# A kernel of attention and capacity-limited MoE: a tail of its own for the last batch, and other PSUM banks for the gather

## The chip, the cores and the metric

One NeuronCore of a Trainium2 chip runs the whole program; the other cores are not used. The metric is the device time of one execution in microseconds (us). Engines are TensorE (PE; its weight loads are shown as PEld), VectorE (DVE), ScalarE (ACT), GpSimd (POOL) and SyncE (SP). Each runs its own queue in order, and semaphores tie them together.

## The reference

For each of 8 batches and 12 heads, attention with squared relu in place of softmax; the heads side by side are `x`. Then, in each batch, the 128 tokens of 448 that score highest against `w_gate` go through a two-layer FFN, and the result, scaled by the sigmoid of the score, is added to their rows.

```python
# q, k, v: (8, 12, 448, 64)
scores = scale * np.matmul(q, k.transpose(0, 1, 3, 2))
attn = np.maximum(scores, 0.0) ** 2 / S
attn_out = np.matmul(attn, v)
x = np.ascontiguousarray(attn_out.transpose(0, 2, 1, 3)).reshape(B, S, H * D)   # (8, 448, 768)

scores = np.einsum('bsd,d->bs', x, w_gate)
out = x.copy()
for b in range(B):
    top_idx = np.argpartition(-scores[b], capacity)[:capacity]                  # capacity 128
    xe = x[b, top_idx]
    h = np.maximum(xe @ w1, 0.0)                                                # w1: 768 x 1024
    ye = h @ w2                                                                 # w2: 1024 x 768
    g = 1.0 / (1.0 + np.exp(-scores[b, top_idx]))
    out[b, top_idx] = x[b, top_idx] + g[:, None] * ye
```

## The kernel before

A tile `t` is one pair of heads of one batch: 48 tiles, six a batch (`t = 6*b + hp`). Inputs are loaded on the GpSimd queue two batches ahead, cast to bf16 on the way. For each tile TensorE transposes q and k into `t_ps`, VectorE copies them out (`qkt`, L172); TensorE makes four chunks of scores (`s_ps`, L182 and L186), ScalarE takes the relu (`r_sb`, L194), VectorE squares it (`a_sb`, L195); TensorE multiplies by v (`o_ps`, L206), one tile behind the scores, and ScalarE writes the result as one of six slices of `xT_sb` (L212), the batch's x with its features on the partitions.

The MoE of a batch is cut into steps that are placed between the attention work of later batches. Two tables give the places: there are twelve half steps `hs` a batch, two a tile. `RANK` serves batch b-1 while batch b's attention runs, `FFN` serves batch b-2. The schedule is written out by hand: each engine executes its instructions in the order in which the Python code issues them. The rank steps are:

- `gate`: six matmuls with `w_gate` repeated, into `sc_ps`, and ScalarE's copy to `bc` (the scores, in all partitions).
- `columns`: four tiny matmuls into `col_ps`, VectorE's copy `cols`, and four small VectorE operations that split each score into three bf16 pieces (`tok`).
- `x_chunk(c)`: six transposes of x into `x_ps` and VectorE's copy to `x_sb`, four times; after the fourth GpSimd issues the write of the batch's `x_sb` to `out`.
- `rank_chunk(c)`: a VectorE instruction with an accumulator counts how many scores are larger (L266), four times.
- `one_hot`: `hot`, a 0/1 matrix of token against rank (L271).
- `select`: four matmuls into `sel_ps`, then VectorE's `sel`, `idx` (the chosen tokens) and `g` (their scores).
- `gather(half)`: 12 matmuls of `x_sb` with `hot` into `xe_ps`, and ScalarE's cast to `xeT`, twice.

The FFN steps are `hidden(f)`, 8 times six matmuls into `h_ps` with a ScalarE relu to `hT` after every fourth; and `project(half, ...)`, 8 matmuls into `ye_ps` and ScalarE's scaling by `g` into `gye`. After the second half GpSimd issues an indirect DMA that adds `gye` to the chosen rows of `out` (the scatter, L328).

[...] `s_ps` has two tiles of two banks each; `t_ps`, `o_ps`, `ma_ps` and `mb_ps` have one bank each. A bank that is written again must first have been read by whoever used it last. The MoE has `ma` (all rank steps, and the first half of the gather) and `mb` (the second half of the gather, and the whole FFN).

All DMAs of the kernel are issued by GpSimd. Writes to `out` follow one another strictly, each waiting until the one before has landed: x of batch b, scatter of batch b-1, x of batch b+1, and so on; at the end the scatter of batch 6 and that of batch 7 stand one behind the other.

Behind the 48 tiles the last attention is done (`attend(NT - 1, c)`), then `moe(B, hs)` for the twelve half steps, which are the rank steps of batch 7 mixed with the FFN of batch 6 by the same tables, and at last the FFN of batch 7 alone.

Of the kernel before, what the change touches and what calls it, by code (L numbers as in the profile page):

```python
# [8 lines left out]
FP32 = mybir.dt.float32  # L9
BF16 = mybir.dt.bfloat16  # L10
# [10 lines left out]
def kernel(  # L21
# [132 lines left out]
    def transposes(t):  # L154
        b, hp = divmod(t, NHP)
        h0 = 2 * hp
        qs, ks = q_sb[b % NBUF], k_sb[b % NBUF]
        ps = t_ps_pool.tile([128, S + 512], BF16, name="t_ps")
        for c in range(NC):
            for hh in range(2):  # L160
                nc.tensor.matmul(out=ps[64 * hh:64 * hh + 64, c * P:(c + 1) * P],  # L161
                                 lhsT=qs[:, h0 + hh, c, :], rhs=ident[:P, :P],
                                 is_transpose=True, start=(c == 0), stop=False,
                                 skip_group_check=True)
        for c in range(4):
            for hh in range(2):
                nc.tensor.matmul(out=ps[64 * hh:64 * hh + 64, S + c * 128:S + (c + 1) * 128],  # L167
                                 lhsT=ks[:, h0 + hh, c, :], rhs=ident,
                                 is_transpose=True, start=False, stop=(c == 3),
                                 skip_group_check=True)  # L170
        sb = qt_pool.tile([128, S + 512], BF16, name="qkt")
        nc.vector.tensor_copy(out=sb, in_=ps)  # L172
        qkt[t] = sb

    def scores(t, c):
        sb = qkt[t]
        ps = s_ps_pool.tile([128, 2, 512], FP32, name="s_ps")
# [20 lines left out]
    def attend(t, c):  # L198
        b, hp = divmod(t, NHP)
        vs = v_sb[b % NBUF]  # L200
        if c == 0:
            o_ps[t] = o_ps_pool.tile([128, S], FP32, name="o_ps")
# [15 lines left out]
    def moe_rank(b):  # L218
        xTb = xT.pop(b)
# [23 lines left out]
        def columns():  # L243
# [5 lines left out]
            nc.vector.tensor_copy(out=cols, in_=col_ps)  # L249
            nc.vector.tensor_copy(out=tk[:, :, 2], in_=cols)  # L250
# [24 lines left out]
        def select():  # L275
            sel_ps = ma_ps_pool.tile([CAP, 5], FP32, name="sel_ps", tag="m")
# [8 lines left out]
        def gather(half):  # L285
            xe = (ma_ps_pool, mb_ps_pool)[half].tile([128, 3, CAP], FP32, name="xe_ps", tag="m")
# [6 lines left out]

        steps = {
            "gate": gate, "col": columns, "x": x_chunk, "rank": rank_chunk,
# [4 lines left out]
    def moe_ffn(b, idx, g, xeT):  # L300
# [4 lines left out]
        def hidden(f):  # L305
            if f % 4 == 0:
                ps["h"] = mb_ps_pool.tile([128, 4, CAP], FP32, name="h_ps", tag="m")
# [7 lines left out]
        def project(half, f0, f1):  # L315
            cols_d = slice(half * 384, half * 384 + 384)
            if f0 == 0:
                ps["y"] = mb_ps_pool.tile([CAP, 384], FP32, name="ye_ps", tag="m")
                if half == 0:
                    nc.scalar.activation(out=g, in_=g, func=AF.Sigmoid)  # L320
# [3 lines left out]
            if f1 == NF:  # L324
                nc.scalar.activation(out=gye[:, cols_d], in_=ps["y"], func=AF.Copy,  # L325
                                     scale=g[:, 0:1])
                if half == 1:
                    nc.gpsimd.indirect_dma_start(  # L328
                        out=out.rearrange("b s d -> (b s) d"),
                        out_offset=bass.IndirectOffsetOnAxis(ap=idx[:, :1], axis=0),  # L330
                        in_=gye, in_offset=None, element_offset=b * S * HD,
                        compute_op=ALU.add)

        return {"h": hidden, "y": project}


# [4 lines left out]
        1: [("gate", 0, 6)], 2: [("col",)], 3: [("x", 0)], 4: [("x", 1), ("rank", 0)],  # L341
# [25 lines left out]
    with tc.manual_schedule():  # L367
        transposes(0)
        transposes(1)
        for t in range(NT):  # L370
# [17 lines left out]
            moe(b, 2 * hp + 1)  # L388
        for c in (0, 1, 3, 2):
            attend(NT - 1, c)  # L390
        for hs in range(12):
            moe(B, hs)
        ffn_steps[B - 1] = moe_ffn(B - 1, *handed.pop(B - 1))
        for hs in range(12):
            place(FFN, ffn_steps[B - 1], hs)
# [35 lines left out]
```

## Time and profile before

| | us |
|---|---|
| median of 3 runs | 269.62 (269.57 to 269.96) |
| profiled execution | 268.7 |
| its span, first to last instruction | 266.6 |
| TensorE busy | 211.8 (79%) |
| ScalarE busy | 196.1 (74%) |
| VectorE busy | 179.8 (67%) |
| GpSimd busy | 88.2 (33%) |

The profile is of one execution, and its instructions' times are counted from the start of the span. No engine is busy all the time, so the shares of busy time do not name the bound. The views to read are the chain of work that ended last, the list of waits in the steady part, and the engines' instructions in order of time at the places that the change touches: one boundary between batches (203 to 216 us) and the tail (from 233 us). An entry such as `[0.81 <-DVE sel L280]` says that the engine stood idle for 0.81 us just before, and that a VectorE instruction of line 280 ended the wait. A matmul's length includes its pipeline: of a row with many, the length divided by the count is near the time from one to the next.

### The profile page before, as it was taken

Reading aid. Unit: us, or ns where it says so; the run is one execution under the profiler, and the core shown is the slowest. Engines: PE = TensorE matmul, PEld = TensorE weight load, DVE = VectorE, ACT = ScalarE, POOL = GpSimd, SP = SyncE. Lnnn points to the kernel's source line nnn. Section 1 sums busy time; section 2 is a strip of 40 time slices with the busy share of each in tenths; the row PEclk is TensorE's granted clock in tenths of the full one; section 3 lists DMA queues with packets and bytes.
Section 4 is the critical chain, followed back from the end, with each engine's and each line's share of the span. In section 5 each row is a group of like instructions: output and inputs, shape, how many; then the busy total and the mean of one; then the engine's idle time right before and its main releaser. Section 6 shows DMA issues by size and latency. Waiting matters only on the chain.

```text
span 266.6 us, 6187 instructions
## 1 busy us (share of the span) xinstructions
PE 211.8 (79%) x2496; PEld 126.8 (48%) x2496; DVE 179.8 (67%) x426; ACT 196.1 (74%) x306; POOL 88.2 (33%) x128
## 2 busy tenths in 40 slices
PE   1297740797798988899889988998899889888740
PEld 1143310253466545565556555655565556366620
DVE  3067850289958976798679867986798669847100
ACT  1088960288988998899889988998899889952320
POOL 8999500955630003700460046002000200020210
PEclk9999985589999999999999999999999999999995
DMA  3999999999999123994499249924202420242544
GB/s 40 104 153 122 174 208 200 144 194 198 208 292 192 16 102 111 149 193 117 134 161 190 96 136 166 186 93 137 47 2 81 138 52 0 115 114 42 207 59 59
DMA packets 41723, 34.20 MB, mean 128 GB/s; under 512 B 14944, under 2 KB 39008, under 8 KB 40800
## 3 DMA queue, kind: packets, MB, share of 16 engines
q0 software_dynamic: 41696, 33.83, 75.9%
q8 instruction: 19, 0.31, 0.4%
q14 instruction: 8, 0.07, 0.1%
HBM read 39.32 MB, written 14.16 MB: 201 GB/s over the span
## 4 chain that ended last, share of the span: by engine, by line
DVE 33%; PE 25%; ACT 14%; DMA 11%; POOL 8%; issue 5%; POOLq 1%; ACTq 0%
DVE a_sb L195 15%; ACT r_sb L194 12%; DMA k_sb<-in_k_dram 7%; DVE qkt L172 7%; DVE trash L266 5%; PE xe_ps L290 5%; PE h_ps L309 4%; PE s_ps L182 4%; DVE x_sb L261 4%; PE sc_ps L238 4%; PE o_ps L206 3%; DMA out_dram<-gye,idx 2%; DMA q_sb<-in_q_dram 2%; POOL k_sb L90 2%; POOL k_sb L93 2%
## 5 line engine op out<-in xcount | busy, mean ns | idle before, releaser
L194 ACT ACTIVATE r_sb<-s_ps 128x896 bf16<-128x896 f32 x192 | 147.4, 830 | 28.4 <-PE s_ps L186 14.8
L195 DVE TENSOR_TENSOR a_sb<-r_sb 128x896 bf16<-128x896 bf16 x192 | 104.3, 563 | 38.8 <-ACT r_sb L194 38.5
L182 PE MATMUL s_ps<-qkt 64*128 64x448 bf16 x288 | 47.2, 368 | 7.7 <-ACT r_sb L194 7.5
L206 PE MATMUL o_ps<-a_sb,v_sb 128*64 128x448 bf16 x384 | 49.7, 369 | 1.3 <-DVE a_sb L195 0.3
L172 DVE COPY qkt<-t_ps 128x960 bf16<-128x960 bf16 x48 | 31.2, 650 | 20.7 <-PE t_ps L167 20.7
L161 PE MATMUL t_ps<-ident,q_sb 112*64 112x112 bf16 x384 | 19.1, 221 | 19.1 <-DMA q_sb<-in_q_dram 13.6
L206 PEld LDWEIGHTS <-v_sb 128*64 128x64 bf16 x384 | 20.0, 111 | 28.2 <-issue 21.7
L263 POOL DMA_DIRECT2D out_dram<-x_sb x8 | 4.5, 564 | 86.5 <-DVE x_sb L261 84.6
L161 PEld LDWEIGHTS <-q_sb 112*64 112x64 bf16 x384 | 17.0, 115 | 26.1 <-DMA q_sb<-in_q_dram 18.8
L212 ACT ACTIVATE xT_sb<-o_ps 128x448 bf16<-128x448 f32 x48 | 26.8, 559 | 1.4 <-PE o_ps L206 1.4
L328 POOL DMA_INDIRECT out_dram<-gye,idx x8 | 13.2, 1653 | 43.6 <-ACT xeT L292 26.9
L309 PE MATMUL h_ps<-xeT,w_sb 128*128 128x128 bf16 x384 | 26.5, 219 | 1.3 <-ACT hT L313 0.7
L182 PEld LDWEIGHTS <-qkt 64*128 64x128 bf16 x288 | 11.4, 94 | 32.1 <-issue 29.5
L93 POOL DMA_DIRECT2D v_sb<-in_v_dram x22 | 16.8, 766 | 29.4 <-DMA q_sb<-in_q_dram 20.7
L322 PE MATMUL ye_ps<-w_sb,hT 128*128 128x384 bf16 x128 | 23.5, 327 | 2.1 <-ACT gye L325 1.1
L309 PEld LDWEIGHTS <-w_sb 128*128 128x128 bf16 x384 | 22.6, 98 | 5.1 <-issue 3.2
L167 PE MATMUL t_ps<-ident,k_sb 128*64 128x128 bf16 x384 | 21.2, 228 | 2.4 <-DMA k_sb<-in_k_dram 2.4
L90 POOL DMA_DIRECT2D v_sb<-in_v_dram x22 | 18.7, 848 | 11.0 <-DMA w_sb<-in_moe_w_dram 7.3
L266 DVE SCALAR_TENSOR_TENSOR trash<-bc,cols,tie 112x448 bf16<-112x448 f32 x32 | 21.6, 676 | 0.0
L258 PE MATMUL x_ps<-ident,xT_sb 128*112 128x128 bf16 x192 | 16.8, 223 | 5.4 <-DVE cols L249 5.3
L313 ACT ACTIVATE hT<-h_ps 128x512 bf16<-128x512 f32 x16 | 9.6, 597 | 13.4 <-PE h_ps L309 13.4
L93 POOL DMA_DIRECT2D k_sb<-in_k_dram x22 | 19.0, 865 | 0.4 <-issue 0.4
(54 smaller groups left out, 214.3 us busy)
## 6 DMA issues: line engine op xcount, KB each, us to landing
out_dram<-x_sb POOLq DMA_DIRECT2D x8, 1344.0 KB, 5.2
q_sb<-in_q_dram POOLq DMA_DIRECT2D x6, 672.0 KB, 10.3
w_sb<-in_moe_w_dram POOLq DMA_DIRECT2D x2, 1536.0 KB, 14.8
k_sb<-in_k_dram POOLq DMA_DIRECT2D x12, 192.0 KB, 10.4
v_sb<-in_v_dram POOLq DMA_DIRECT2D x12, 192.0 KB, 7.8
k_sb<-in_k_dram POOLq DMA_DIRECT2D x12, 144.0 KB, 10.3
v_sb<-in_v_dram POOLq DMA_DIRECT2D x12, 144.0 KB, 10.4
q_sb<-in_q_dram POOLq DMA_DIRECT2D x2, 224.0 KB, 4.2
```

Of the source, the lines that this page charges most:

```text
L90: nc.gpsimd.dma_start(out=t[0:64, hs, 0:lo, :], in_=src[b, hs, 0:64 * lo].rearrange("h (p c) d -> p h c d", c=lo))
L93: nc.gpsimd.dma_start(out=t[64:128, hs, 0:hi, :], in_=src[b, hs, 64 * lo:S].rearrange("h (p c) d -> p h c d", c=hi))
L161: nc.tensor.matmul(out=ps[64 * hh:64 * hh + 64, c * P:(c + 1) * P], lhsT=qs[:, h0 + hh, c, :], rhs=ident[:P, :P], is_transpose=True, start ...
L172: nc.vector.tensor_copy(out=sb, in_=ps)
L182: nc.tensor.matmul(out=ps[:, hh, :S], lhsT=sb[rows, S + c * 128:S + (c + 1) * 128], rhs=sb[rows, :S], start=True, stop=True)
L194: nc.scalar.activation(out=r[:, :n], in_=ps[:, :n, :S], func=AF.Relu)
L195: nc.vector.tensor_tensor(out=a[:, :n], in0=r[:, :n], in1=r[:, :n], op=ALU.mult)
L206: nc.tensor.matmul(out=o_ps[t][rows, :], lhsT=vs[:, 2 * hp + hh, c, :], rhs=a[:, hh if c < 3 else 0, :], start=(c == 0), stop=(c == 2), sk ...
L212: nc.scalar.activation(out=xT[b][:, hp, :], in_=o_ps.pop(t), func=AF.Copy, scale=o_scale)
L266: nc.vector.scalar_tensor_tensor(out=trash, in0=bc[:P, :], scalar=cols[:, c:c + 1], in1=tie[:, c, :], op0=ALU.subtract, op1=ALU.is_ge, acc ...
L309: nc.tensor.matmul(out=ps["h"][:, f % 4, :], lhsT=w1_sb[:, m, f * 128:(f + 1) * 128], rhs=xeT[:, m, :], start=(m == 0), stop=(m == NM - 1))
L322: nc.tensor.matmul(out=ps["y"], lhsT=hT[:, f, :], rhs=w2_sb[:, f, cols_d], start=(f == 0), stop=(f == NF - 1))
```

## The change

It has three parts.

1. In every batch, `gather` swaps its banks: the first half goes into `mb`, the second into `ma`. Tags are added so that other tiles can share the pools `t_ps`, `s_ps` and `o_ps`; this alone changes nothing. `columns` is split into `columns` and `pieces`, which the table still places together.
2. The tail is written out by hand. TensorE does five of the six gate matmuls and 20 of the 24 x transposes of batch 7 (`x_begin`, into the two `s_ps` tiles) ahead of the last attention, and the sixth gate matmul, the columns and the last four transposes (`x_end`) behind it. VectorE does the four rank instructions and the one-hot in a row, `pieces` after them. `x_sb` is copied by ScalarE in two large pieces instead of by VectorE in four. Batch 6's FFN follows, its `h` in `mb` and `t`, its `y` in `mb` and `ma`; the gather of batch 7 (`gather_last`, into `o` and `t`, one half cast by each of ScalarE and VectorE) stands between the two `y`, and `select` comes last, into `o`.
3. The FFN of batch 7 (`last`) has its own code: both `h` halves in `s_ps` tiles, the first three feature blocks of four hidden blocks ahead of the other three, the two `y` halves in different banks and interleaved by the halves of `hT`, and the final scaling shared by ScalarE and VectorE.

```diff
@@ moe_rank
-        xTb = xT.pop(b)
+        xTb = xT[b]
...
             nc.vector.tensor_copy(out=cols, in_=col_ps)
+
+        def pieces():
             nc.vector.tensor_copy(out=tk[:, :, 2], in_=cols)
...
-        def select():
-            sel_ps = ma_ps_pool.tile([CAP, 5], FP32, name="sel_ps", tag="m")
+        def select(pool=ma_ps_pool, tag="m"):
+            sel_ps = pool.tile([CAP, 5], FP32, name="sel_ps", tag=tag)
...
         def gather(half):
-            xe = (ma_ps_pool, mb_ps_pool)[half].tile([128, 3, CAP], FP32, name="xe_ps", tag="m")
+            xe = (mb_ps_pool, ma_ps_pool)[half].tile([128, 3, CAP], FP32, name="xe_ps", tag="m")
...
+        def x_begin():
+            for i in range(2):
+                ps["x", i] = s_ps_pool.tile([P, 2, 1024], BF16, name="x_ps2", tag="s")
+                for u in range(2):
+                    for m in range(NM - 1):
+                        x_part(i, u, m)
+
+        def x_part(i, u, m):
+            c = 2 * i + u
+            nc.tensor.matmul(out=ps["x", i][:, u, m * 128:(m + 1) * 128],
+                             lhsT=xTb[:, m, c * P:(c + 1) * P], rhs=ident,
+                             is_transpose=True, start=(m == 0), stop=(m == NM - 1))
+
+        def x_end():
+            for i in range(2):
+                for u in range(2):
+                    x_part(i, u, NM - 1)
+                nc.scalar.copy(out=x_sb[:, 2 * i:2 * i + 2, :], in_=ps["x", i][:, :, :HD])
+            nc.gpsimd.dma_start(out=out[b].rearrange("(p c) d -> p c d", c=NC), in_=x_sb)
+
+        def gather_last():
+            for half, (pool, tag) in enumerate(((o_ps_pool, "o"), (t_ps_pool, "t"))):
+                xe = pool.tile([128, 3, CAP], FP32, name="xe_ps2", tag=tag)
+                for mm in range(3):
+                    m = half * 3 + mm
+                    for c in range(NC):
+                        nc.tensor.matmul(out=xe[:, mm, :], lhsT=x_sb[:, c, m * 128:(m + 1) * 128],
+                                         rhs=hot[:, c, :], start=(c == 0), stop=(c == NC - 1))
+                (nc.scalar.copy if half == 0 else nc.vector.tensor_copy)(
+                    out=xeT[:, half * 3:half * 3 + 3, :], in_=xe)
@@ moe_ffn
+        def last():
+
+            nc.scalar.activation(out=g, in_=g, func=AF.Sigmoid)
+            for half in range(2):
+                h = s_ps_pool.tile([128, 4, CAP], FP32, name="h_ps2", tag="s")
+                for m0 in (0, 3):
+                    for ff in range(4):
+                        f = 4 * half + ff
+                        for m in range(m0, m0 + 3):
+                            nc.tensor.matmul(out=h[:, ff, :],
+                                             lhsT=w1_sb[:, m, f * 128:(f + 1) * 128],
+                                             rhs=xeT[:, m, :], start=(m == 0 and ff == 0),
+                                             stop=(m == NM - 1), skip_group_check=True)
+                f = 4 * half
+                nc.scalar.activation(out=hT[:, f:f + 4, :], in_=h, func=AF.Relu)
+            y = [mb_ps_pool.tile([CAP, 384], FP32, name="y_ps2", tag="m"),
+                 t_ps_pool.tile([CAP, 384], FP32, name="y_ps3", tag="t")]
+            for f0 in (0, 4):
+                for half in range(2):
+                    for f in range(f0, f0 + 4):
+                        nc.tensor.matmul(out=y[half], lhsT=hT[:, f, :],
+                                         rhs=w2_sb[:, f, half * 384:half * 384 + 384],
+                                         start=(f == 0), stop=(f == NF - 1))
+            nc.scalar.activation(out=gye[:, :384], in_=y[0], func=AF.Copy, scale=g[:, 0:1])
+            nc.vector.tensor_scalar(out=gye[:, 384:], in0=y[1], scalar1=g[:, 0:1],
+                                    scalar2=None, op0=ALU.mult)
+            scatter()
@@ behind the 48 tiles
+        last, prev = B - 1, B - 2
+        r, handed[last] = moe_rank(last)
+        f = moe_ffn(prev, *handed.pop(prev))
+        r["gate"](0, NM - 1)
+        r["x_begin"]()
         for c in (0, 1, 3, 2):
             attend(NT - 1, c)
-        for hs in range(12):
-            moe(B, hs)
-        ffn_steps[B - 1] = moe_ffn(B - 1, *handed.pop(B - 1))
-        for hs in range(12):
-            place(FFN, ffn_steps[B - 1], hs)
+        r["gate"](NM - 1, NM)
+        r["col"]()
+        for c in range(NC):
+            r["rank"](c)
+        r["hot"]()
+        r["x_end"]()
+        for i in range(8):
+            f["h"](i, *((mb_ps_pool, "m"), (t_ps_pool, "t"))[i // 4])
+        f["y"](0, 0, 8, mb_ps_pool)
+        r["pieces"]()
+        r["xe_last"]()
+        f["y"](1, 0, 8, ma_ps_pool)
+        r["sel"](o_ps_pool, "o")
+        moe_ffn(last, *handed.pop(last))["last"]()
```

On TensorE, at the end of each batch's rank work, the gather follows the last scores of a tile. Before (LDWEIGHTS are the weight loads; `[waits DVE_49]` is a wait for VectorE, here for the `sel` copy):

```order
L182 LDWEIGHTS qkt
L182 MATMUL s_ps<-qkt 128x448
L290 LDWEIGHTS x_sb
L290 MATMUL xe_ps<-hot,x_sb 128x128 [waits DVE_49]
L290 LDWEIGHTS x_sb
L290 MATMUL xe_ps<-hot,x_sb 128x128
```

Now the same place, the twelfth and thirteenth of the 24 matmuls among it:

```order
L182 LDWEIGHTS qkt
L182 MATMUL s_ps<-qkt 128x448
L292 LDWEIGHTS x_sb
L292 MATMUL xe_ps<-hot,x_sb 128x128
...
L292 MATMUL xe_ps<-hot,x_sb 128x128
L292 LDWEIGHTS x_sb
L292 MATMUL xe_ps<-hot,x_sb 128x128 [waits DVE_49]
```

The wait for VectorE moved from the first gather matmul to the thirteenth, the first of the second half.

On TensorE at the last attention (`o_ps`), before: it follows the gather of batch 6 at once, and the gate of batch 7 comes behind it.

```order
L290 MATMUL xe_ps<-hot,x_sb 128x128
L206 LDWEIGHTS v_sb_99
L206 MATMUL o_ps<-a_sb,v_sb_99 64x448 [waits Activation_49]
...
L309 MATMUL h_ps<-xeT,w_sb 128x128 [waits Activation_49]
...
L238 MATMUL sc_ps<-xT_sb,wg_rep 128x448
L238 LDWEIGHTS wg_rep
L238 MATMUL sc_ps<-xT_sb,wg_rep 128x448 [waits Activation_49]
```

Now:

```order
L292 MATMUL xe_ps<-hot,x_sb 128x128
L238 LDWEIGHTS wg_rep
L238 MATMUL sc_ps<-xT_sb,wg_rep 128x448 [waits Activation_49]
...
L306 MATMUL x_ps_4128<-ident,xT_sb 112x128
...
L306 MATMUL x_ps_4139<-ident,xT_sb 112x128
L206 LDWEIGHTS v_sb_99
L206 MATMUL o_ps<-a_sb,v_sb_99 64x448
...
L238 MATMUL sc_ps<-xT_sb,wg_rep 128x448 [waits Activation_49]
L246 MATMUL col_ps<-one_f,bc 112x1 [waits Activation_49]
```

Five gate matmuls, the first of them waiting for ScalarE's cast of the gather, and 20 transposes moved ahead of the attention; only the sixth gate matmul is left behind it.

On ScalarE, from the casts of batch 6's gather to the end, before:

```order
L292 CAST xeT<-xe_ps 128x384 [waits PE_49] x2
L212 ACTIVATE xT_sb<-o_ps 128x448 [waits PE_49]
L241 COPY bc<-sc_ps 128x448 [waits PE_49]
L313 ACTIVATE hT<-h_ps 128x512 [waits PE_49] x2
L320 ACTIVATE g<-g 128x1 [waits DVE_49]
L325 ACTIVATE gye<-ye_ps,g 128x384 [waits DMASW0_49,PE_49,Activation_49]
L325 ACTIVATE gye<-ye_ps,g 128x384 [waits PE_49]
L292 CAST xeT<-xe_ps 128x384 [waits PE_49] x2
L313 ACTIVATE hT<-h_ps 128x512 [waits PE_49] x2
```

Now:

```order
L294 CAST xeT<-xe_ps 128x384 [waits PE_49] x2
L212 ACTIVATE xT_sb<-o_ps 128x448 [waits PE_49]
L241 COPY bc<-sc_ps 128x448 [waits PE_49]
L314 COPY x_sb<-x_ps_4128 112x1536 [waits DMASW4_49,DMASW7_49,DMASW2_49,PE_49]
L314 COPY x_sb<-x_ps_4139 112x1536 [waits PE_49]
L348 ACTIVATE hT<-h_ps 128x512 [waits PE_49] x2
L355 ACTIVATE g<-g 128x1 [waits DVE_49]
L360 ACTIVATE gye<-ye_ps,g 128x384 [waits DMASW0_49,PE_49,Activation_49]
L325 CAST xeT<-xe_ps_4247 128x384 [waits PE_49]
L360 ACTIVATE gye<-ye_ps,g 128x384 [waits PE_49]
```

The two copies of `x_sb` moved in ahead of batch 6's relus `hT`, and one cast of `xeT` went to VectorE. (`DMASW` names the completion of DMAs of earlier batches; `x_ps_4128` and `x_ps_4139` are the two tiles of `x_begin`.)

## Rows read from the trace of the kernel before

**Rows 1.** The page's part 4: chain that ended last, by engine
```profile
DVE 33%; PE 25%; ACT 14%; DMA 11%; POOL 8%; issue 5%; POOLq 1%; ACTq 0%
```

**Rows 2.** Waits, 70 to 232 us: engine, line, releaser, total us, times, longest
```profile
PE xe_ps L290 <- DVE sel L280: 4.9, 6, 0.8
ACT xeT L292 <- PE xe_ps L290: 4.7, 12, 0.6
```

**Rows 3.** TensorE in order of time, one boundary: start, length, operation [idle before <-releaser]
```profile
207.94 1.50 PE L290 MATMUL xe_ps<-hot,x_sb 112*128 112x128 bf16 x24 [0.81 <-DVE sel L280]
```

**Rows 4.** ScalarE, the same boundary
```profile
208.80 0.48 ACT L292 CAST xeT<-xe_ps 128x384 bf16<-128x384 f32 x1 [0.58 <-PE xe_ps L290]
...
209.85 1.73 ACT L194 ACTIVATE r_sb<-s_ps 128x896 bf16<-128x896 f32 x2
```

**Rows 5.** VectorE, the same boundary
```profile
207.73 0.15 DVE L280 COPY sel<-sel_ps 128x5 f32<-128x5 f32 x1
...
210.81 0.63 DVE L195 TENSOR_TENSOR a_sb<-r_sb 128x896 bf16<-128x896 bf16 x1 [1.76 <-ACT r_sb L194]
```

**Rows 6.** All engines in order of time, the last attention and the gate behind it
```profile
234.02 1.50 PE L290 MATMUL xe_ps<-hot,x_sb 112*128 112x128 bf16 x24 [0.37 <-DVE sel L280]
...
234.89 0.48 ACT L292 CAST xeT<-xe_ps 128x384 bf16<-128x384 f32 x1
...
235.45 0.95 PE L206 MATMUL o_ps<-a_sb,v_sb 128*64 128x448 bf16 x8
...
236.44 0.55 ACT L212 ACTIVATE xT_sb<-o_ps 128x448 bf16<-128x448 f32 x1 [0.40 <-PE o_ps L206]
236.52 1.59 POOL L328 DMA_INDIRECT out_dram<-gye,idx  x1 [5.33 <-ACT xeT L292]
...
236.68 1.30 PE L238 MATMUL sc_ps<-xT_sb,wg_rep 128*128 128x448 bf16 x6
...
238.01 0.53 ACT L241 COPY bc<-sc_ps 128x448 f32<-128x448 f32 x1 [1.03 <-PE sc_ps L238]
...
239.01 0.16 DVE L249 COPY cols<-col_ps 112x4 f32<-112x4 f32 x1 [3.44 <-PE col_ps L246]
```

**Rows 7.** All engines in order of time, the tail
```profile
245.09 0.56 DVE L261 COPY x_sb<-x_ps 112x768 bf16<-112x768 bf16 x1 [0.99 <-PE x_ps L258]
...
245.57 0.68 DVE L266 SCALAR_TENSOR_TENSOR trash<-bc,cols,tie 112x448 bf16<-112x448 f32 x1
245.95 0.58 POOL L263 DMA_DIRECT2D out_dram<-x_sb  x1 [7.84 <-DVE x_sb L261]
...
246.29 0.69 DVE L271 TENSOR_TENSOR hot<-slot_row,rank 112x512 bf16<-112x512 f32 x1
...
249.61 1.50 PE L309 MATMUL h_ps<-xeT,w_sb 128*128 128x128 bf16 x24 [0.57 <-ACT xeT L292]
...
251.78 1.58 POOL L328 DMA_INDIRECT out_dram<-gye,idx  x1 [5.26 <-ACT hT L313]
...
253.98 1.46 PE L322 MATMUL ye_ps<-w_sb,hT 128*128 128x384 bf16 x8 [0.69 <-ACT hT L313]
...
257.66 0.58 ACT L325 ACTIVATE gye<-ye_ps,g 128x384 f32<-128x384 f32 x1 [1.55 <-PE ye_ps L322]
258.70 1.56 POOL L328 DMA_INDIRECT out_dram<-gye,idx  x1 [5.34 <-ACT gye L325]
```

**Rows 8.** Groups by line and shape: count | busy us, mean ns | idle before, releaser
```profile
L194 ACT ACTIVATE r_sb<-s_ps 128x896 bf16<-128x896 f32 x144 | 126.3, 922 | 12.7 <-PE s_ps L182 12.2
...
L194 ACT ACTIVATE r_sb<-s_ps 128x448 bf16<-128x448 f32 x48 | 26.6, 554 | 15.6 <-PE s_ps L186 14.8 <-PE s_ps L182 0.4
```

**Rows 9.** DMA issues, 245 to 253 us: KB, median us to landing
```profile
out_dram<-x_sb POOLq DMA_DIRECT2D x1, 1344.0 KB, 5.1
out_dram<-gye,idx POOLq DMA_INDIRECT x1, 5.6
```

**Rows 10.** The page's part 2: granted TensorE clock, 40 slices of 6.7 us
```profile
PEclk9999985589999999999999999999999999999995
```

More of the change, by code (lines that the diff above doesn't have):

```diff
@@ L157, in transposes @@
         qs, ks = q_sb[b % NBUF], k_sb[b % NBUF]
-        ps = t_ps_pool.tile([128, S + 512], BF16, name="t_ps")
+        ps = t_ps_pool.tile([128, S + 512], BF16, name="t_ps", tag="t")
         for c in range(NC):
@@ L176, in scores @@
         sb = qkt[t]
-        ps = s_ps_pool.tile([128, 2, 512], FP32, name="s_ps")
+        ps = s_ps_pool.tile([128, 2, 512], FP32, name="s_ps", tag="s")
         s_ps[t, c] = ps
@@ L201, in attend @@
         if c == 0:
-            o_ps[t] = o_ps_pool.tile([128, S], FP32, name="o_ps")
+            o_ps[t] = o_ps_pool.tile([128, S], FP32, name="o_ps", tag="o")
         a = a_sb.pop((t, c))
@@ L292, in gather @@
             nc.scalar.copy(out=xeT[:, half * 3:half * 3 + 3, :], in_=xe)
+        def x_begin():
[25 more added lines that the diff above has]
+                    out=xeT[:, half * 3:half * 3 + 3, :], in_=xe)
         steps = {
-            "gate": gate, "col": columns, "x": x_chunk, "rank": rank_chunk,
+            "x_begin": x_begin, "x_end": x_end, "xe_last": gather_last,
+            "gate": gate, "col": columns, "pieces": pieces, "x": x_chunk, "rank": rank_chunk,
             "hot": one_hot, "sel": select, "xe": gather,
@@ L303, in moe_ffn, with hidden @@
         ps = {}
-        def hidden(f):
+        def hidden(f, pool=mb_ps_pool, tag="m"):
             if f % 4 == 0:
-                ps["h"] = mb_ps_pool.tile([128, 4, CAP], FP32, name="h_ps", tag="m")
+                ps["h"] = pool.tile([128, 4, CAP], FP32, name="h_ps", tag=tag)
             for m in range(NM):
@@ L313, in hidden, with project @@
                 nc.scalar.activation(out=hT[:, f - 3:f + 1, :], in_=ps["h"], func=AF.Relu)
-        def project(half, f0, f1):
+        def project(half, f0, f1, pool=mb_ps_pool):
             cols_d = slice(half * 384, half * 384 + 384)
             if f0 == 0:
-                ps["y"] = mb_ps_pool.tile([CAP, 384], FP32, name="ye_ps", tag="m")
+                ps["y"] = pool.tile([CAP, 384], FP32, name="ye_ps", tag="m")
                 if half == 0:
@@ L327, in project @@
                 if half == 1:
[L328 to L334, printed above, removed]
+                    scatter()
[24 more added lines that the diff above has]
+                                    scalar2=None, op0=ALU.mult)
+            scatter()
@@ L340, with scatter @@
+        def scatter():
+            nc.gpsimd.indirect_dma_start(
+                out=out.rearrange("b s d -> (b s) d"),
+                out_offset=bass.IndirectOffsetOnAxis(ap=idx[:, :1], axis=0),
+                in_=gye, in_offset=None, element_offset=b * S * HD, compute_op=ALU.add)
+        return {"h": hidden, "y": project, "last": last}
     RANK = {
-        1: [("gate", 0, 6)], 2: [("col",)], 3: [("x", 0)], 4: [("x", 1), ("rank", 0)],
+        1: [("gate", 0, 6)], 2: [("col",), ("pieces",)], 3: [("x", 0)], 4: [("x", 1), ("rank", 0)],
```

## The prediction

> **What bounds the kernel now.** I began with the chain of work that ended last [rows 1]: no engine owns it. VectorE, TensorE and ScalarE hand it to one another, so a single wait can lie on it. Next the waits between 70 and 232 us, the steady part [rows 2]: the gather `xe_ps` on TensorE waits six times for VectorE's `sel` copy, 0.8 us each, and ScalarE's casts `xeT` wait 4.7 us for the gather. Then one batch boundary by engine [rows 3 to 5]. TensorE stands idle for 0.81 us, until 207.94. ScalarE idles 0.58 us before the first cast and starts the next tile's relu at 209.85. VectorE has 1.76 us of slack before its next square, so it is not a second limit. In these rows the reader is to see one pattern: everything after the gather moves with the gather.
>
> Last the tail [rows 6, 7]. Its end is a chain of writes to `out` that must not overlap: batch 7's `x_sb` is written at 245.95, batch 6's scatter starts at 251.78, batch 7's at 258.70. The first two steps are set by `x_sb` and by a landing; the last start waited for `gye` (257.66 + 0.58 = 258.24), 0.5 us after the earlier scatter alone would have let it go. From 258.70 to the span's end, 266.6, are 7.9 us that nothing here touches.
>
> **Part 1, the banks of the gather, in every batch.** Today the gather's first half takes the bank of `sel_ps` and so waits for the `sel` copy. After the change the first half takes the other bank, free since the earlier `gye`, and only the second half waits. TensorE idles 0.81 us before 207.94 [rows 3], so the first half can start at 207.13. Twelve matmuls at 1.50/24 = 0.06 us end by 207.9, about when `sel` is copied (207.73 + 0.15 [rows 5]); the second half then starts at 207.94 with 12 matmuls to go instead of 24. TensorE gains 12 x 0.06 = 0.7 us. ScalarE can follow: its waits for the gather are 4.7/6 = 0.78 us a batch [rows 2], so its relu starts at about 209.15 instead of 209.85. The next wait there is the second half for `sel`, near nothing. The other side of the swap is the next batch: its `hidden` now uses the bank cast first and its gate the bank cast second, each asked for only behind the next tile's scores and attention: free.
>
> The gain holds only if TensorE, ScalarE and VectorE all shift, and they do. Loads are issued two batches ahead, and in the view of [rows 2] no engine but GpSimd waits for one. Per batch the ends are 0.58 us (the first cast's idle time alone) and 0.78 us (all of it); I take 0.68, nearest the 12 matmuls. Six boundaries: **4.1 us**, from 3.5 to 4.7. The seventh, worth 0.37 us [rows 6], is inside the tail.
>
> **Part 2, the tail, on the old time axis.** First what is moved ahead of the last attention: five of six gate matmuls and 20 of 24 x transposes, in the TensorE queue. The gather starts at 234.02 - 0.37 = 233.65 and ends at 235.15. The gate's bank is now that of the gather's second half, so TensorE waits for its cast: the first cast still runs at 234.89, the second ends at about 235.8. This is a new wait of 0.7 us, and queued behind it are the transposes and the whole last attention. Five gate matmuls at 1.30/6 = 0.2 us: 236.8. Twenty transposes, priced like the `h_ps` matmuls of the same shape, 1.50/24 = 0.06 us [rows 7]: 238.0. So the attention starts at 238.0 instead of 235.45, **2.55 us late**. From its start to its cast `xT_sb` is 0.99 us [rows 6], the cast takes 0.55, the sixth gate matmul 0.4: `bc` starts at 240.0 against 238.01. The early gate saves only what stood behind the attention, and it costs more ahead of it: net 2.0 us late here.
>
> That is earned back behind it. `cols` is copied 1.16 us after `bc` starts (238.01 to 239.01 + 0.16 [rows 6]): 241.2. The four rank instructions, at 0.72 us start to start (245.57 to 246.29 [rows 7]), now run with nothing between them: the one-hot starts at 244.1 instead of 246.29. Beside them, from 241.25, ScalarE copies `x_sb` in two pieces of 1536 elements. No row shows this form. ScalarE's rows give 554 ns at 448 and 922 ns at 896 elements, a slope of 0.82 ns, so 1.45 us at 1536; VectorE's copy of 768 16-bit elements takes 560 ns, so 1536 at that pace take about 1.1 us [rows 7, 8]. I take 1.45 as it is ScalarE's own line, with a 0.1 us overlap of the two: `x_sb` is ready at 244.0, against 245.09 + 0.56 = 245.65.
>
> [...]
>
> The write leaves 0.3 us behind the copy, as now (245.65 to 245.95): 244.3, **1.65 us earlier**. Ahead of it in the GpSimd queue is only batch 5's scatter, started at 236.52 and landed 5.6 us later, at 242.1 [rows 6, 9]. From this write to batch 6's scatter are 251.78 - 245.95 = 5.83 us, of which 5.1 are the landing [rows 7, 9]: 250.15. From scatter to scatter: 5.6 to land and 0.7 to start, as behind the write: 256.45.
>
> Is the arithmetic ready? Batch 6's `hidden` (48 x 0.06 us) runs during the copies, but its two relus queue behind them on ScalarE: 244.0 to 245.1. Its first projection, the 24 gathers and its second projection follow without a gap on TensorE and end at 248.7; `gye` lands at 249.3, ready for a scatter at 249.8. That is 0.35 us before the write allows it. Batch 7's two `hidden` halves (2.8 us behind `sel`) and 16 projections (1.46 us for 8, end to end 2.6) end at 254.1; VectorE's scaling of 384 elements, at most the 0.68 us of a rank instruction on 448, taken as 0.6, ends at 254.7, ready for 255.1. That is 1.3 us before the landing allows it. So the landings set the end, and the separate banks of the last FFN are hidden at nothing; uncovered, each would be worth a wait like the 0.57 us ahead of 249.61 [rows 7].
>
> The last scatter starts at 256.45 against 258.70: **2.2 us**. Bounds: with copies of 1.1 us the write goes 0.7 us sooner, but then `gye` is last: gain 3.0. With ScalarE slower by the same amount: 1.5. With half a microsecond more at the new wait: 1.0.
>
> **Sum.** 4.1 + 2.2 = 6.3 us: the span of 266.6 becomes 260.3, and the profiled execution of 268.7 becomes 262.4. The median shown is 0.9 above that execution, so 269.6 - 6.3 = **263.3 us**. The bounds give 4.5 to 7.7, that is 265.1 to 261.9.
>
> **Rivals.** *A, the loop gains and the tail does not.* The new wait and the in-order queue ahead of the attention cost a further 2 us, or ScalarE's copies hold batch 6's relus longer. For it: 2.0 of delay at the gate is already in my sum. Against: `x_sb` must slip from 244.0 to 246. 265.5 us.
> *B, the tail gains and the loop does not.* Some other path as long as the gather's would have to cross each boundary. Against: the idle times in [rows 2, 4, 5] leave room of 0.7 us on each engine. 267.4 us.
> *C, neither moves*: another wait of 0.7 us takes the place of `sel` and A holds too. 269.6 us.
> *D, slower: the TensorE clock.* Five gates and 20 transposes come in a row, and if the clock fell to its half from 238 us on, the path's 14 us of matmuls would take up to 14 more. The scaling at 254.7 has 1.3 us of cover, the tail's 2.2 and the loop's 4.1: beyond 7.6 us, so with over half of this work at the lower clock, the kernel is slower; with three quarters 272.5 us. [...]
> [...]
>
> **Chances.** Forecast 0.68, A 0.15, B 0.09, C 0.04, D 0.04. What a measurement can tell from no change is about 0.2%, 0.5 us. Faster: the forecast, A and B, 0.92; within 0.2%: 0.04; slower: 0.04. The range takes the bounds of the forecast and reaches to A: 261.8 to 265.6; left out are B, C, D and a little at the ends.
>
> **What would show it.** In the loop: no `xe_ps` wait for `sel` over 0.1 us and a batch period shorter by 0.7 us. In the tail: ScalarE's two `x_sb` copies near 1.45 us each, batch 6's scatter 5.8 us behind the write of `x_sb`, the last scatter about 6.3 us behind that, and its release by a landing rather than by `gye`. I am wrong if the loop's period stays, if the copies are far from 1.45 us, or if the last scatter waits for the arithmetic.

## The result, and the profile after

Median of four runs: 263.57 us (263.47 to 264.09) after the change, 269.69 us (269.57 to 269.96) before; the ratio is 0.9775, with a 95% interval of 0.9759 to 0.9792. The forecast was 263.3. The profiled execution took 263.62 us, its span 261.8 us.

The waits of the kernel after, 70 to 232 us, in the columns of [rows 2]:

```profile
PE x_ps L260 <- DVE cols L249: 4.4, 6, 0.7
...
ACT xeT L294 <- PE xe_ps L292: 1.3, 6, 0.2
```

The gather's wait for `sel` is no longer in the list (before 4.9 us), and ScalarE's wait for the gather fell from 4.7 to 1.3 us. What is left on TensorE is an old wait, for the rank columns. One boundary between batches, all engines in order of time, which answers to [rows 3 to 5]:

```profile
204.33 1.72 PE L292 MATMUL xe_ps<-hot,x_sb 112*128 112x128 bf16 x24
...
205.01 0.16 DVE L282 COPY sel<-sel_ps 128x5 f32<-128x5 f32 x1
...
205.38 0.49 ACT L294 CAST xeT<-xe_ps 128x384 bf16<-128x384 f32 x1
...
206.08 0.48 ACT L294 CAST xeT<-xe_ps 128x384 bf16<-128x384 f32 x1 [0.22 <-PE xe_ps L292]
```

The gather begins 0.68 us ahead of `sel` with no idle time before it. It lasts 1.72 us instead of 1.50, since its second half still waits 0.2 us for the copy.

The tail of the kernel after, all engines in order of time. Its axis is 3.39 us ahead of the one before (batch 6's x write starts at 227.22, before at 230.61), so 3.39 is added for a comparison with the prediction's times:

```profile
230.20 1.51 PE L292 MATMUL xe_ps<-hot,x_sb 112*128 112x128 bf16 x24
...
231.37 0.91 ACT L294 CAST xeT<-xe_ps 128x384 bf16<-128x384 f32 x2
...
232.33 1.10 PE L238 MATMUL sc_ps<-xT_sb,wg_rep 128*128 128x448 bf16 x5 [0.62 <-ACT xeT L294]
...
233.27 1.28 PE L306 MATMUL x_ps<-ident,xT_sb 128*112 128x128 bf16 x20
...
234.48 0.95 PE L206 MATMUL o_ps<-a_sb,v_sb 128*64 128x448 bf16 x8
...
236.45 0.53 ACT L241 COPY bc<-sc_ps 128x448 f32<-128x448 f32 x1 [0.44 <-PE sc_ps L238]
...
237.45 0.16 DVE L249 COPY cols<-col_ps 112x4 f32<-112x4 f32 x1 [5.27 <-PE col_ps L246]
...
237.70 2.78 ACT L314 COPY x_sb<-x_ps 112x1536 bf16<-112x1536 bf16 x2 [0.71 <-PE x_ps L306]
...
240.63 0.69 DVE L273 TENSOR_TENSOR hot<-slot_row,rank 112x512 bf16<-112x512 f32 x1
240.77 0.57 POOL L315 DMA_DIRECT2D out_dram<-x_sb  x1 [6.00 <-ACT x_sb L314]
...
246.82 1.58 POOL L394 DMA_INDIRECT out_dram<-gye,idx  x1 [5.47 <-ACT g L367]
...
250.64 0.62 DVE L389 TENSOR_SCALAR gye<-y_ps,g 128x384 f32<-128x384 f32 x1 [4.88 <-ACT gye L388]
253.64 1.56 POOL L394 DMA_INDIRECT out_dram<-gye,idx  x1 [5.25 <-issue]
```

The last rows of the chain that ended last, kernel after: start, length, what:

```profile
237.70 2.79 ACT x_sb L314 x2
...
240.77 5.17 DMA out_dram<-x_sb
...
246.08 0.74 issue
246.82 5.58 DMA out_dram<-gye,idx
...
252.47 0.94 issue
253.41 1.79 POOLq L505
```

Arithmetic is on this chain up to the x copies, and behind them only transfers: batch 7's `gye` is ready at 251.26, over a microsecond before the earlier scatter lands at 252.40.

The writes of batch 0's and batch 6's `x_sb` bound the six gathers of the loop. GpSimd in order of time, kernel before:

```profile
69.55 0.56 POOL L263 DMA_DIRECT2D out_dram<-x_sb  x1 [1.85 <-DMA k_sb<-in_k_dram]
...
230.61 0.58 POOL L263 DMA_DIRECT2D out_dram<-x_sb  x1 [18.62 <-DVE x_sb L261]
```

The same, kernel after:

```profile
70.18 0.56 POOL L265 DMA_DIRECT2D out_dram<-x_sb  x1 [1.58 <-DMA k_sb<-in_k_dram]
...
227.22 0.58 POOL L265 DMA_DIRECT2D out_dram<-x_sb  x1 [17.71 <-DVE x_sb L263]
```

By the two traces the time went thus (starts of GpSimd's transfers; before, after):

| | before | after | difference |
|---|---|---|---|
| start of the span to batch 0's x write | 69.55 | 70.18 | +0.63 |
| from there to batch 6's x write, six batches | 161.06 | 157.04 | -4.02 |
| to batch 7's x write | 15.34 | 13.55 | -1.79 |
| to batch 6's scatter | 5.83 | 6.05 | +0.22 |
| to batch 7's scatter | 6.92 | 6.82 | -0.10 |
| to the span's end | 7.87 | 8.13 | +0.26 |

The loop gave 4.0 us and the tail 1.4. The first row is no effect of the change: over the profiles of this case it varies from 69.1 to 71.6 us, mostly in kernels that do the same up to there.

### The profile page after: what moved, and what is told of

Same layout as the page of the kernel before. It is cut to its first block, busy times and chain, and to the rows that moved or that the text cites. A ratio compares the mean times of both kernels' runs of the same rounds, so it can differ in the third digit from the quotient of the medians.

```text
span 261.8 us, 6189 instructions
## 1 busy us (share of the span) xinstructions
PE 208.8 (80%) x2496; PEld 125.2 (48%) x2496; DVE 179.7 (69%) x424; ACT 196.8 (75%) x306; POOL 89.0 (34%) x128
## 4 chain that ended last, share of the span: by engine, by line
PE 28%; DVE 27%; ACT 15%; DMA 14%; POOL 8%; issue 5%; POOLq 1%; ACTq 0%
DVE a_sb L195 13%; ACT r_sb L194 12%; DMA k_sb<-in_k_dram 8%; DVE qkt L172 5%; PE s_ps L182 5%; PE sc_ps L238 4%; PE o_ps L206 4%; DVE trash L268 4%; PE xe_ps L292 3%; PE h_ps L344 3%; DVE x_sb L263 3%; DMA q_sb<-in_q_dram 2%; DMA out_dram<-gye,idx 2%; DMA out_dram<-x_sb 2%; POOL k_sb L90 2%
## 5 line engine op out<-in xcount | busy, mean ns | idle before, releaser
L206 PE MATMUL o_ps<-a_sb,v_sb 128*64 128x448 bf16 x384 | 48.2, 359 | 1.3 <-DVE a_sb L195 0.3
L394 POOL DMA_INDIRECT out_dram<-gye,idx x8 | 14.1, 1767 | 44.0 <-ACT r_sb L194 21.5
L265 POOL DMA_DIRECT2D out_dram<-x_sb x7 | 3.9, 560 | 72.7 <-DVE x_sb L263 71.2
L93 POOL DMA_DIRECT2D v_sb<-in_v_dram x22 | 16.7, 760 | 31.1 <-DMA q_sb<-in_q_dram 21.4
L344 PE MATMUL h_ps<-xeT,w_sb 128*128 128x128 bf16 x336 | 23.0, 219 | 0.0
L90 POOL DMA_DIRECT2D v_sb<-in_v_dram x22 | 17.9, 815 | 10.6 <-DMA w_sb<-in_moe_w_dram 6.9
L357 PE MATMUL ye_ps<-w_sb,hT 128*128 128x384 bf16 x112 | 20.6, 327 | 0.6 <-ACT hT L348 0.6
L344 PEld LDWEIGHTS <-w_sb 128*128 128x128 bf16 x336 | 19.6, 98 | 2.8 <-issue 1.2
L260 PE MATMUL x_ps<-ident,xT_sb 128*112 128x128 bf16 x168 | 14.9, 224 | 5.8 <-DVE cols L249 5.8
L93 POOL DMA_DIRECT2D k_sb<-in_k_dram x22 | 18.6, 850 | 0.4 <-issue 0.4
L90 POOL DMA_DIRECT2D k_sb<-in_k_dram x22 | 18.7, 852 | 0.1
```

The lines of the kernel that those rows point to most:

```text
L90: nc.gpsimd.dma_start(out=t[0:64, hs, 0:lo, :], in_=src[b, hs, 0:64 * lo].rearrange("h (p c) d -> p h c d", c=lo))
L93: nc.gpsimd.dma_start(out=t[64:128, hs, 0:hi, :], in_=src[b, hs, 64 * lo:S].rearrange("h (p c) d -> p h c d", c=hi))
L206: nc.tensor.matmul(out=o_ps[t][rows, :], lhsT=vs[:, 2 * hp + hh, c, :], rhs=a[:, hh if c < 3 else 0, :], start=(c == 0), stop=(c == 2), sk ...
L344: nc.tensor.matmul(out=ps["h"][:, f % 4, :], lhsT=w1_sb[:, m, f * 128:(f + 1) * 128], rhs=xeT[:, m, :], start=(m == 0), stop=(m == NM - 1))
```

## The experiments

All kernels were timed against the kernel before on the same chip. Four chips were used, on which the kernel before took 269.0 to 269.4 us, so kernels of different groups are best compared by their ratios. First the kernel after was measured again, on one chip with the first three variants.

> The changed kernel once more, beside the three others. Theory: 263.6 us. For the profile: the first write of x_sb, 70.2 us in the profile of after and 69.6 in that of before, moves by some tenths from run to run, since it hangs on the loads at the start; rival: it is later in the changed kernel every time, and the change costs 0.6 us there.

263.6 us (262.7 to 264.39), ratio 0.9802 (0.9777 to 0.9828), 5.4 us less than before (268.97 on this chip). In its profile the batch period (from the write of one batch's `x_sb` to the next, batches 1 to 5) is 26.08 to 26.10 us and the stretch from batch 6's x write to batch 7's 13.56, as in the first profile. The first x write starts at 69.36, earlier than the 69.55 of the kernel before, so the later start in the first profile of after is no effect of the change, and the span is 260.8 us.

**Each part alone.** Kernel before, with only the gather's banks exchanged:

```diff
-            xe = (ma_ps_pool, mb_ps_pool)[half].tile([128, 3, CAP], FP32, name="xe_ps", tag="m")
+            xe = (mb_ps_pool, ma_ps_pool)[half].tile([128, 3, CAP], FP32, name="xe_ps", tag="m")
```

> The kernel before with one edit: the two halves of the gather swap their banks. Everything else, the tail too, is as before. Theory (loop and tail gain apart, the loop 0.67 us at each of six boundaries): 4.0 us, 265.7 us where before is 269.7, and the first gather matmul no longer waits for the sel copy. Rival (the boundaries give nothing by themselves, the gain of the whole change is the tail's): within 0.5 us of before. Rival (the seventh boundary counts as well, since the old tail starts 0.37 us earlier): 4.4 us.

264.98 us, ratio 0.9857 (0.983 to 0.9883): 4.0 us less. The period fell from 26.74 to 26.10 us, and the stretch from batch 6's x write to batch 7's from 15.34 to 14.94. So the swap gives the loop's whole gain with none of the new tail, and also the seventh boundary, by 0.40 us ([rows 6] show 0.37).

Kernel after, with the old banks (the same line, the other way round):

> The changed kernel with the gather's banks as before, so that only the tail is new. Theory: the part of the gain that the tail has, 1.4 us by the two profiles (last scatter 1.7 us earlier, its landing 0.3 us longer), 2.2 us by the prediction: 267.5 to 268.3 us where before is 269.7. Rival (the parts need one another, as the gate waits for the other half's cast): no gain, 269.7. With e1 the two gains should add up to the whole change's 6.1 us.

267.11 us, ratio 0.993 (0.9914 to 0.9947): 1.9 us less than before, with the old period of 26.75. The two parts add: 4.0 + 1.9 = 5.9 against 6.1 and 5.4 measured together. Here batch 6's x write to batch 7's takes 13.25 us, 0.3 less than in the kernel after: with the old banks the early gate waits for the first cast of the gather only. So the new tail gives away in its gate what the seventh boundary would bring.

**The order at the last attention.** Kernel after, attention first, then the whole gate and the 20 transposes:

```diff
-        r["gate"](0, NM - 1)
-        r["x_begin"]()
         for c in (0, 1, 3, 2):
             attend(NT - 1, c)
-        r["gate"](NM - 1, NM)
+        r["gate"](0, NM)
+        r["x_begin"]()
         r["col"]()
```

> The changed kernel with the early part of the tail undone: the last attention comes first, then the six gate matmuls, then the 20 transposes, then the columns. Theory (gate and transposes ahead of the attention cost 2 us, which only the later steps win back; and the chain of writes to out sets the end): the columns 2.0 us earlier, the write of x_sb 2.0 us earlier, where it meets the landing of batch 5's scatter, and the end 2.0 us earlier: 261.6 us where the changed kernel has 263.6. Rival (the early gate and transposes are what the tail gains from): 1 to 2 us slower than the changed kernel. Rival (the end is set by the arithmetic of batch 7, not by the writes): under 0.5 us of difference.

261.51 us, ratio 0.9738 (0.9715 to 0.9761): 2.1 us less than the kernel after on the same chip by the medians, 1.4 by the profiles (spans 259.4 and 260.8, first x write 69.39 and 69.36). Its tail, all engines in order of time:

```profile
232.44 1.59 POOL L394 DMA_INDIRECT out_dram<-gye,idx  x1 [5.39 <-ACT xeT L294]
...
234.56 0.16 DVE L249 COPY cols<-col_ps 112x4 f32<-112x4 f32 x1 [3.13 <-PE col_ps L246]
...
234.81 2.78 ACT L314 COPY x_sb<-x_ps 112x1536 bf16<-112x1536 bf16 x2 [1.14 <-PE x_ps L306]
...
238.62 0.57 POOL L315 DMA_DIRECT2D out_dram<-x_sb  x1 [4.60 <-ACT hT L348]
```

From batch 6's x write (226.47) to `cols` are 8.09 us instead of 10.23. So the early gate and transposes cost 2.1 us where they stand; the prediction had priced this delay at 2.0. By the trace, only 1.4 of it comes back at the write: `x_sb` is ready at 237.59, but the write starts at 238.62. Batch 5's scatter lands at 238.10, 5.67 us after its start, and the write follows 0.52 us later. The row names ScalarE's `hT` as the releaser, but the write needs no `hT`, and in the last two kernels below it stands 0.52 us behind this landing too: the landing let it go.

**The FFN of the last batch.** Kernel after, with batch 7's FFN by the old steps in one bank:

```diff
-        moe_ffn(last, *handed.pop(last))["last"]()
+        f = moe_ffn(last, *handed.pop(last))
+        for hs in range(12):
+            place(FFN, f, hs)
```

> The changed kernel with the FFN of batch 7 undone: its steps run as the other batches' do, one bank for all, each part waiting until ScalarE has read the part before. In the kernel before, this FFN takes 8.6 us from its first matmul to the end of gye; the new code takes 6.2 us. Theory (the landings of the writes to out set the end, and the new FFN's 2.4 us are mostly cover): gye ends at about 253.7 on the axis of the profile of after, the last scatter starts at 254.2 instead of 253.6, and the end is 0.5 us later, 264.1 us where the changed kernel has 263.6. Rival (the arithmetic of batch 7 sets the end): 2.4 us later, 266.0.

263.5 us, ratio 0.9797 (0.977 to 0.9824), against 263.6 of the kernel after. The end of its tail, all engines in order of time:

```profile
252.62 0.58 ACT L360 ACTIVATE gye<-ye_ps,g 128x384 f32<-128x384 f32 x1 [1.55 <-PE ye_ps L357]
253.67 1.56 POOL L394 DMA_INDIRECT out_dram<-gye,idx  x1 [5.88 <-ACT gye L360]
```

The last scatter now starts 0.47 us behind `gye` (253.20) and 7.46 behind the scatter before it, where the kernel after has 6.82: 0.6 us in the trace, not to be seen in the medians. The new code of the last FFN (its banks, its order and the shared scaling, which this run does not tell apart) takes some 2.5 us of arithmetic away (from batch 6's scatter to `gye` 6.99 us here, 4.44 there), and most of it lies beside a transfer.

**The last scatter's start.** In the kernel after it begins 1.24 us behind the landing that it waits for (252.40 to 253.64); a scatter behind the landing of an x write begins 0.87 us behind it (245.95 to 246.82; 0.77 in the kernel before), and an x write behind a scatter's landing 0.52. (The 0.74 in the two expectations below is the last `issue` row of that 0.87 alone, so it is too low beside the 1.24.) First idea: it is long because nothing follows in GpSimd's queue.

```diff
+    trail = const.tile([P, 1], FP32)
...
             scatter()
+            nc.gpsimd.memset(trail, 0.0)
```

> The changed kernel with one tiny GpSimd memset issued behind the last scatter. In all runs the last scatter starts 1.24 us or more behind the landing of the one before, where the others start 0.74 us behind a landing. Theory (the last instruction of the queue is issued later because it is the last): with another behind it, it starts 0.74 us behind the landing, and the end is 0.5 us earlier, which only the profile can tell. Rival (it belongs to the second of two scatters in a row): 1.24 us as before.

263.62 us, ratio 0.9777 (0.9751 to 0.9802). The scatter before it lands at 253.58 and the last one starts at 254.82: 1.24 again. The idea fell. Second idea: it is long because a scatter directly follows a scatter.

```diff
+    spare = const.tile([P, 1], FP32)
+    seed = const.tile([P, 1], FP32)
+    nc.vector.memset(seed, 0.0)
...
         def last():
+            nc.gpsimd.dma_start(out=spare, in_=seed)
```

> Between the last two scatters GpSimd issues one small transfer (112 rows of 4 bytes, from SBUF to SBUF, that nothing reads and that waits for nothing late). Theory: the long 1.24 us from the landing of batch 6's scatter to the start of batch 7's belongs to an indirect transfer that directly follows another in GpSimd's queue; with the small one between, it falls to the 0.74 us that a scatter behind a direct write shows. Rival: it belongs to waiting for the landing of a scatter rather than of a direct write, and stays at 1.24 us. The total moves by 0.5 us or less in either case.

GpSimd in order of time, this kernel:

```profile
246.63 1.58 POOL L397 DMA_INDIRECT out_dram<-gye,idx  x1 [5.45 <-ACT g L370]
247.69 1.13 POOL L369 DMA_DIRECT2D spare<-seed  x1
252.91 1.60 POOL L397 DMA_INDIRECT out_dram<-gye,idx  x1 [4.09 <-DMA out_dram<-gye,idx]
```

The chain that ended last, the same kernel:

```profile
246.63 5.46 DMA out_dram<-gye,idx
252.10 0.02 issue
252.12 0.04 POOLq L397
252.16 0.52 issue
```

From the landing at 252.10 to the start are 0.81 us instead of 1.24, near the 0.87 of a scatter behind an x write. So the wait for a scatter's landing is not enough for the long start: it goes with a scatter that directly follows another. Whether it takes a direct transfer between them, or whether any instruction of GpSimd would do, was not tested, and what GpSimd does in the additional 0.4 us no view shows. One run of 263.02 us says nothing of the total.

**The wait that is left in the loop.** One boundary of the kernel after, all engines in order of time, at the rank columns:

```profile
187.46 0.15 DVE L249 COPY cols<-col_ps 112x4 f32<-112x4 f32 x1
...
187.67 0.49 PE L260 MATMUL x_ps<-ident,xT_sb 128*112 128x128 bf16 x6 [0.73 <-DVE cols L249]
...
188.00 0.83 PE L344 MATMUL h_ps<-xeT,w_sb 128*128 128x128 bf16 x12
...
188.87 0.60 ACT L348 ACTIVATE hT<-h_ps 128x512 bf16<-128x512 f32 x1 [0.83 <-PE h_ps L344]
```

The first x transposes want the bank of `col_ps`, and behind them in TensorE's queue stand the FFN matmuls on which ScalarE waits. It is the same pattern as the gather's. First attempt: in the table, the first two x steps stand one half step later, the third stays, and the last stands one half step earlier.

```diff
-        1: [("gate", 0, 6)], 2: [("col",), ("pieces",)], 3: [("x", 0)], 4: [("x", 1), ("rank", 0)],
-        5: [("rank", 1)], 6: [("x", 2)], 7: [("rank", 2)], 8: [("x", 3), ("rank", 3)],
+        1: [("gate", 0, 6)], 2: [("col",), ("pieces",)], 4: [("x", 0), ("rank", 0)],
+        5: [("x", 1), ("rank", 1)], 6: [("x", 2)], 7: [("x", 3), ("rank", 2)], 8: [("rank", 3)],
```

> The changed kernel with one edit in the table of the loop: the first transposes of x stand half a step later, the second one step, and the last half a step earlier, with the same work in all. In the changed kernel TensorE waits 0.73 us in each of six batches ahead of the first x transposes, because VectorE has not yet read the columns out of the same bank; behind the half step it has. Theory (a wait of TensorE for a bank just ahead of work that ScalarE waits for is worth its length, as at the gather): 0.4 to 0.7 us a batch, 2.4 to 4.2 us in all, 259.4 to 261.2 where the changed kernel has 263.6. Rival (only the gather's wait was on the path; the others have slack behind them): within 0.5 us of 263.6. The tail is the same but for the earlier write of batch 6's x_sb, which moves nothing while the later writes wait for x_sb of batch 7.

274.68 us, ratio 1.019 (1.0168 to 1.0213): 11 us slower than the kernel after. The waits of this kernel, 70 to 232 us:

```profile
PE x_ps L260 <- DVE x_sb L263: 11.0, 11, 1.3
```

And one batch, all engines in order of time:

```profile
198.51 0.50 PE L260 MATMUL x_ps<-ident,xT_sb 128*112 128x128 bf16 x6 [0.80 <-DVE x_sb L263]
...
200.38 0.60 ACT L348 ACTIVATE hT<-h_ps 128x512 bf16<-128x512 f32 x1 [1.58 <-PE h_ps L344]
...
204.34 0.49 PE L260 MATMUL x_ps<-ident,xT_sb 128*112 128x128 bf16 x6 [1.25 <-DVE x_sb L263]
...
206.22 0.58 ACT L360 ACTIVATE gye<-ye_ps,g 128x384 f32<-128x384 f32 x1 [1.86 <-issue]
```

One wait of 0.73 us became two of 0.80 and 1.25 a batch, now for the copy of the x step one half step earlier, and both stand ahead of FFN matmuls. The period rose from 26.08 to 28.06 us. ScalarE's waits add to about as much: ahead of these `hT` and `gye` they are 1.58 and 1.86 us, and at the corresponding places of the kernel after 0.83 and 0.29 (`hT` at 188.87 and 193.06) and 0.31 (`gye` at 197.52), 2.0 us less. The expectation had not asked when the x steps, now in four half steps in a row, get their bank back from one another. The same table with the attention put first gave no other answer for the loop:

> The last attention ahead of the gate and the transposes, and the x transposes later in the table, together. Theory (the loop's waits and the tail's chain add up): the loop's gain of the run with the table alone, and the 2 us of the run with the attention first, the latter a little more, as batch 6's x_sb is now written half a step earlier and batch 5's scatter lands before batch 7's x_sb is ready: 256.5 to 259.5 us. Rival (the loop gives nothing): 261 us.

272.7 us, ratio 1.0127 (1.0103 to 1.0151), period 28.06; 2.0 us less than without the attention put first.

Second attempt: the table stays, and at half step 3 alone the FFN's two hidden parts go ahead of the transposes.

```diff
-            if hs >= 1:
+            if hs >= 1 and hs != 3:
                 place(RANK, rank_steps[b - 1], hs)
         if b >= 2:
...
             place(FFN, ffn_steps[b - 2], hs)
+        if b >= 1 and hs == 3:
+            place(RANK, rank_steps[b - 1], hs)
```

> At half step 3 of every loop batch, the second two of the FFN's four hidden parts go ahead of the first x transposes of the rank step; nothing else moves. Theory: the 0.73 us for which TensorE waits for the rank columns (4.4 us in 6) goes, as the columns are long read, and no new wait comes, since the transposes stand 0.67 us later and not two half steps later: 0.6 to 0.7 us a batch, six batches, 259.4 to 260.0 us. Rival: the wait only moves to the next step of ScalarE or VectorE, as it did where the x steps were put later: within 0.5 us of 263.6, or slower.

259.64 us (258.71 to 260.18), ratio 0.9636 (0.9604 to 0.9668): the theory's number. The same place in this kernel, all engines in order of time:

```profile
184.63 0.84 PE L344 MATMUL h_ps<-xeT,w_sb 128*128 128x128 bf16 x12
...
185.23 0.15 DVE L249 COPY cols<-col_ps 112x4 f32<-112x4 f32 x1
...
185.43 0.49 PE L260 MATMUL x_ps<-ident,xT_sb 128*112 128x128 bf16 x6
...
185.68 0.60 ACT L348 ACTIVATE hT<-h_ps 128x512 bf16<-128x512 f32 x1
```

The transposes start when `cols` has just been copied, with no idle time, and `hT` has lost its 0.83 us too. The period is 25.36 us, 0.72 less. With the attention put first as well:

> The same move at half step 3 together with the last batch's attention ahead of its gate transposes. Theory: the two gains stand in different stretches and add, some 2 us in the tail and 3.6 to 4.2 in the loop: 257.5 to 258.5 us. Rival: the loop gives nothing, and the time is that of the attention put first alone, 261.5 us.

257.4 us (256.85 to 258.0), ratio 0.9563 (0.9531 to 0.9595): the gains add. With the small transfer between the last scatters in addition:

> The move at half step 3, the last attention first, and the small transfer between the last two scatters. Theory: the three gains add; the last scatter starts about 0.8 us behind the landing of the one before instead of 1.24, 0.4 us less than the 257.4 us of the first two together: 257.0 us. Rival: the arithmetic or something else behind the landing takes its place, and the time stays at 257.4 us or above. The timed medians alone can hardly tell these apart, so the start behind the landing decides.

257.42 us, ratio 0.9554 (0.9528 to 0.958). The last scatter starts 0.81 us behind the landing (246.34 to 247.15), as forecast, and 6.22 us behind the scatter before it instead of 6.73. But in this profile batch 5's scatter took 6.00 us to land instead of 5.61, which holds the x write back, and from the last scatter to the span's end are 8.16 us instead of 7.94. Whether the half microsecond is real in the total, these runs can't tell. The best kernel of the study is thus either of the two, 12 us below the kernel before.

## Why the prediction was right, point by point

**The loop, 0.68 us a batch and 4.1 in all: right.** 0.67 a batch, 4.02 in all. The swap alone gave it, so its cause is shown and not only argued: rivals B and C fall. It came from TensorE's 12 matmuls as reasoned, and the three engines shifted together. One sign missed its bound: the second half still waits 0.2 us for `sel`, where under 0.1 was said.

**The tail up to the x write: right in nearly every step.** With the 3.39 us added, forecast and measured: gather 233.65 and 233.59; the early gate's new wait 0.7 and 0.62; attention 238.0 and 237.87; `bc` 240.0 and 239.84; one-hot 244.1 and 244.02; `x_sb` ready 244.0 and 243.88; its write 244.3 and 244.16; batch 6's scatter 250.15 and 250.21; `gye` 254.7 and 254.65.

**The two ScalarE copies: right, and the disputed price is settled.** They took 2.78 us together, 1.44 each, against 1.45 from ScalarE's own line in [rows 8]. The 1.1 us at VectorE's pace did not come.

**The last scatter: the mis-sized term.** I read its start in [rows 7] as held by `gye`, 0.5 us behind what the landing alone would allow, and took 0.7 us from a landing to a start. In the new tail `gye` is early, and the start still stands 1.24 us behind the landing; before it was 1.37 (257.33 to 258.70). So `gye` had cost 0.13 us there, and the step of this term that failed is the price of a start taken from another pair of transfers. Measured on the common axis: 257.03, not 256.45. I also let the end stay at 7.9 us, and it was 8.1 here; over all profiles it varies from 7.9 to 8.2. Together the tail gave 1.4 us by the trace instead of 2.2, 1.9 by the medians of the variant with the old banks. The new code of the last FFN, which I had put at nothing, is worth 0.6 us at the last scatter's start: without it `gye` is last.

**That the total is so near is partly luck.** 4.0 + 1.4 = 5.4 us by the trace and 6.1 by the medians of the first comparison, 5.4 by those of the second. The starts of the executions differ by about as much as the tail was mis-sized. For the profiled execution itself I had 262.4 us, and it took 263.62.

**Rival A** (the loop alone) did not come: `x_sb` would have had to slip to 246, and it is ready at 243.88. The 2 us of delay at the early gate that speak for it are real, and I had them in the sum, but saw in them only a price and not a part to leave out. **Rival D** did not come either: with 20 transposes in a row (233.27 to 234.55) the granted clock is full, 1.00, in every stretch read from 55 to 255 us. The page's clock line of the kernel after, in tenths of full speed (9 is 90% or more):

```profile
PEclk9999995589999999999999999999999999999995
```

It is half only in two stretches, as in [rows 10]: 0.50 from 42 to 54 us, around a wait for loads, where TensorE stood idle for 10.3 us until 47.09, and 0.50 from 256 us to the end, behind its last matmul, which ended at 250.53. The kernel before could already say something of this: it has 22 transposes in a row, and the granted clock there is 1.00 from 192 to 195 us. TensorE in order of time, kernel before:

```profile
192.76 0.36 PE L161 MATMUL t_ps<-ident,q_sb 112*64 112x112 bf16 x8
192.96 0.39 PE L167 MATMUL t_ps<-ident,k_sb 128*64 128x128 bf16 x8
193.28 0.54 PE L258 MATMUL x_ps<-ident,xT_sb 128*112 128x128 bf16 x6
```

That a row of transposes lowers the clock is not shown by any run here: 20 and 22 of them between other matmuls left the granted clock at 1.00.

## What to carry to other kernels

Where a step in an in-order queue waits for a bank, look first at what stands behind it in the queue: here two exchanges of neighbours, banks at the gather and FFN ahead of transposes at half step 3, gave about 4 us each, while moving the same transposes to other half steps cost 11. Work that is done early is only early for itself: five gate matmuls and 20 transposes ahead of the last attention made the columns 2.1 us late, and with them behind it the end came 1.4 us (by the traces) to 2.1 us (by the medians) sooner. And the price of a start is to be taken from the same pair of transfers, since what releases it in the profile's brackets may not be what it waited for last.

## What the runs showed of the hardware that I had not expected

- An indirect DMA that directly follows another in GpSimd's queue started 1.24 us behind the landing that it waited for (252.40 to 253.64 in the kernel after), in nine of the ten profiles of the new tail without anything between (in the tenth it waited for `gye`); with a small direct DMA between them, 0.81 us (252.10 to 252.91 and 246.34 to 247.15), in both profiles that have one.
- The time from the start of the span to the first x write varied from 69.1 to 71.6 us over the profiles of this case, and from 69.4 to 70.2 between two profiles of the one kernel after. Differences below a microsecond are better read from a stretch of the trace than from a span.
